# Quarter 2 of g in the last batch turned by TensorE instead of through DRAM

## The chip, the cores and the metric

One core of one Trainium2 chip runs the whole program. The metric is device time in microseconds (us): the median of several executions. One further execution ran under the hardware profiler, and every row below is from it.

## The reference, cut to what matters

Attention between tokens and a small state, a dense feed-forward layer with a piecewise activation, and a mixture of eight experts over 32 soft slots:

```python
attn = concat([softmax(x @ state.T / 8) @ state, softmax(state @ x.T / 8) @ x])   # 8 x 8 heads, 512 tokens, 32 state rows
x = attn.reshape(4352, 512)
h = x @ w_in                                                # 2048 features
g = where(h >= 1, h, where(h <= -1, 0, (h + 1) ** 2 / 4))
y = g @ w_out
logits = y @ phi                                            # 32 slots
slot_in = softmax(logits, over tokens).T @ y
slot_out = relu(slot_in @ w1[e]) @ w2[e]                    # expert e has 4 slots
out = softmax(logits, over slots) @ slot_out
```

## The kernel before

The work goes by batches b = 0 to 7 of 512 tokens each; a ninth pass, b = 8, takes the 256 state rows of all batches. In each batch `hstep` (L430) runs 16 steps m. A step makes h of 128 features x 512 tokens by six matmuls (L445; in b = 8 twelve of half the width, L453), and ScalarE, GpSimd and VectorE make g of it (the last instruction of a step is VectorE's L497). Four steps are a quarter of g: quarter k is steps 4k to 4k + 3.

g is used twice. `estep` (L554) multiplies a quarter by wp, the product of w_out and phi, into E, the logits. `smblock` (L564) makes of E the token weights dN and then, quarter by quarter, F = dN times g (L632), which VectorE adds to acc (L641). For F the tokens have to lie on the partitions, so g has to be turned, and there are two ways to do it.

The way through DRAM is `tstep` (L529). VectorE turns blocks of 32 x 32 into a buffer gD, one instruction a step (L534). After a quarter's fourth step SP issues four writes of 256 KB to DRAM (gdr, L541) and one read-back of 1 MB into nat (L543). The read-back waits in SP's queue for the writes to land, and what stands behind it waits with it.

The way by TensorE is `tquarter` (L518): 16 transposes of 128 x 128 against the identity into four PSUM tiles (gtp, L523), and four copies by ScalarE into nat or, for quarter 3, into the freed gD0.

`by_pe` (L514) says which way a quarter goes: in batches 1 to 6 all four go through DRAM; in b = 7, the last full batch, those in `CFG["pe"]` go by TensorE, here quarter 3 alone. F of b = 7 is computed during b = 8, and its quarters stand in TensorE's order between matmuls of h.

```python
def by_pe(b, c):
    return b == B or b == 0 and c not in CFG["tqv"] or b == B - 1 and c in CFG["pe"]

# in the loop, for the step mt before this one
if not by_pe(bt, mt // 4):
    tstep(bt, mt)
elif mt % 4 == 3:
    tquarter(bt, mt // 4)
```

Buffers that are no longer needed are given (L748) to loads of the experts' weights w1 (16 loads of 1 MB) and w2 (16 more). w1_0 to w1_5 go from GpSimd's queue, all later ones from SP's. gD has three buffers in turn; the third, gD2, lies in the slot wb1, which is given to w1_7. In b = 7 quarter 0 uses gD0, quarter 1 gD1 and quarter 2 gD2.

After b = 8 follow the merged slots (SI, L931), the experts' first layer (L950, reads w1), the second (SO, L983, reads w2, in two halves of eight groups), and the output: SR (L991) spreads a half of the slot outputs, and tiles `ops` (L1008) of three matmuls each are evicted, some by VectorE (L1004), some by ScalarE, and written by 16 transfers of 512 KB and 16 small ones.

The order is made by a scheduler when the program is built, except that TensorE's instructions from b = 2 up to the end of b = 7 stand as written; which of them run ahead in b = 8 and in the output is the scheduler's choice.

Of the kernel before, what the change touches and what calls it, by code (L numbers as in the profile page):

```python
# [14 lines left out]
PE = mybir.EngineType.PE  # L15


CFG = dict(hp=2000, att7=(3, 5, 6, 7, 8, 10), og=1, n3=1, n3m=12, wS=['DP', 'AD', 'AD', 'AD', 'AD', 'DP', 'AD', 'DD', 'AD', 'AD', 'AD', 'AD', 'AD', 'AD', 'AD', 'AD'], xsm=13, k0=5, rg=6, spg=0, att0=6, att=7, V0=(2, 6, 10), Vn=(0, 4, 10), Vx=12, wn='H', wsev='adad', conv=(1, 2, 3, 4, 12, 13, 19, 21, 24, 26, 28, 32, 36, 40, 44, 48, 52, 56, 60), todo=[1, 1, 1, 2, 0, 0, 0, 3, 0, 0, 2, 2, 1, 1, 0, 0], E0=2, E=1, sm=1, tqB=(5, 9, 13), GP=10, pe=(3,), psH=3, gtpX=(0, 7), tq0=(13, 15), keep=(2, 3, 4, 5), x2=(1, 1), natm=1, warm=14, bounce7=None, split=1, wt=4, so='sscscscscscscscc', smm=(1, 2, 3, 4, 5, 6, 9), tqv=(), tqvm=0, first='x', apath=2, f32c=1, place=1, attm=(3, 6, 7, 8, 9, 12), subPm=True, loDm=False, bounce=(0, 1, 2, 3), bq=('s', 's'), xq='s', nat=((1, 11), (2, 2), (2, 3), (2, 11), (3, 2), (3, 4), (3, 9), (4, 2), (4, 3), (4, 9), (5, 2), (5, 3), (5, 9), (6, 2), (6, 4), (6, 9)), subP=(), mulD=(0, 1), loD=(0, 1), qlag=0, gv0='SSSSSSSSSSSSSSSS', gv='EEESEEESEEESEEES', gvS='BBBBBBBBBBBBBBBB')


@with_exitstack
def kernel(
# [20 lines left out]
    def pool(name, bufs, **kw):  # L43
        return ctx.enter_context(tc.tile_pool(name=name, bufs=bufs, **kw))
# [6 lines left out]
    small = pool("small", 2)  # L51
    psH = pool("psH", CFG["psH"], space=PSUM)
    psE = pool("psE", 1, space=PSUM)
    psV = pool("psV", 1, space=PSUM)
    psX = pool("psX", 5 - CFG["psH"], space=PSUM)
    dram = pool("dram", 1, space=bass.MemoryType.DRAM)
# [25 lines left out]
    def slot(name, tag=None, dt=F32):  # L82
        return slots.tile([128, 2048], dt, name=name, tag=tag or name)
# [8 lines left out]

    v_s = [slot(f"v{c}", dt=F32R) if c or not CFG["f32c"] else None for c in range(2)]
    a_st = slot("ast", tag="a1")
# [27 lines left out]
    def group(calls, after=()):  # L122

        first = mm(**calls[0])  # L124
        for i in after:
            tc.add_manual_dep(first.ins, i.ins.name, SYNC, reason="side by side")
        with tc.high_priority(CFG["hp"]):
            for c in calls[1:]:
# [26 lines left out]
    def convert(src, dst, tmp):  # L155

        w = src.bitcast(U32).rearrange("p (f w) -> p f w", w=2)
        lo, hi, d = w[:, :, 0], w[:, :, 1], dst.bitcast(U32)
        nc.vector.tensor_scalar(out=d, in0=hi, scalar1=0x07FFFFFF, scalar2=3,
                                op0=ALU.bitwise_and, op1=ALU.logical_shift_left)  # L160
        nc.vector.scalar_tensor_tensor(out=d, in0=hi, scalar=0xC0000000, in1=d,
                                       op0=ALU.bitwise_and, op1=ALU.bitwise_or)
        if tmp is None:
            nc.vector.scalar_tensor_tensor(out=d, in0=lo, scalar=29, in1=d,
                                           op0=ALU.logical_shift_right, op1=ALU.bitwise_or)
        else:
            t = tmp.bitcast(U32)

            act(tmp, lo, ACTF.Relu, scale=-2.0 ** -29, bias=seven)
            act(t, tmp, ACTF.Relu, scale=-1.0, bias=seven)  # L170
            nc.vector.tensor_tensor(out=d, in0=d, in1=t, op=ALU.bitwise_or)

    def piece(i, k, dst):
        rot["t"] += 1
        tmp = None if rot["t"] in CFG["conv"] else cw_t[rot["t"] % 3]
        convert(stage[i][:, 1024 * k:1024 * k + 1024], dst, tmp)
# [33 lines left out]
    def load_x(b):  # L210
        (dma if CFG["xq"] == "s" or b < 3 else nc.gpsimd.dma_start)(out=xs_s, in_=xs[b])

# [873 lines left out]
```

## Time and profile before

| | |
|---|---|
| median of three runs | 518.12 us (517.38 to 519.41) |
| the profiled execution | 520.69 us |
| its span in the trace | 518.5 us |
| mean granted clock of TensorE | 0.944 of full speed |
| busy share of the span: TensorE, VectorE, ScalarE, GpSimd | 89%, 71%, 60%, 40% |
| HBM traffic | 100.34 MB read, 41.42 MB written |

Times in the rows are us from the span's start unless marked ns. PE is TensorE (PEld its weight loads), DVE VectorE, ACT ScalarE, POOL GpSimd, SP the engine that only issues transfers (SPq its queue). L445 is line 445. `out<-in` are the program's names, `x6` a count, and brackets at a row's end give the idle time ahead of it and what ended that.

### The profile page before, as it was taken

Reading aid. Unit: us, or ns where it says so; the run is one execution under the profiler, and the core shown is the slowest. Engines: PE = TensorE matmul, PEld = TensorE weight load, DVE = VectorE, ACT = ScalarE, POOL = GpSimd, SP = SyncE. Lnnn points to the kernel's source line nnn. Section 1 sums busy time; section 2 is a strip of 40 time slices with the busy share of each in tenths; the row PEclk is TensorE's granted clock in tenths of the full one; section 3 lists DMA queues with packets and bytes.
Section 4 is the critical chain, followed back from the end, with each engine's and each line's share of the span. In section 5 each row is a group of like instructions: output and inputs, shape, how many; then the busy total and the mean of one; then the engine's idle time right before and its main releaser. Section 6 shows DMA issues by size and latency. Waiting matters only on the chain.

```text
span 518.5 us, 9979 instructions
## 1 busy us (share of the span) xinstructions
PE 462.9 (89%) x3757; PEld 267.5 (52%) x3757; DVE 369.0 (71%) x768; ACT 313.4 (60%) x613; POOL 209.5 (40%) x211
## 2 busy tenths in 40 slices
PE   5382999999989999999998998999999769799994
PEld 2130465566545555555565455556457548335583
DVE  2999798869568879969968987985896745310370
ACT  0778997677667667767766866866656426211242
POOL 0000000045527776776776776877573100110041
PEclk9685999999999999999999999999999979989965
DMA  8998072546449797697596877789589898899998
GB/s 314 420 419 362 6 317 84 164 163 181 145 163 332 268 292 247 205 322 253 197 314 201 283 265 239 274 284 336 185 277 353 322 398 323 301 385 418 385 298 292
DMA packets 40127, 142.39 MB, mean 275 GB/s; under 512 B 3984, under 2 KB 12560, under 8 KB 27920
## 3 DMA queue, kind: packets, MB, share of 16 engines
q1 hardware_dynamic: 38400, 133.91, 72.5%
q0 software_dynamic: 1680, 7.87, 4.4%
q8 instruction: 29, 0.48, 0.4%
q14 instruction: 18, 0.15, 0.1%
HBM read 100.34 MB, written 41.42 MB: 273 GB/s over the span
## 4 chain that ended last, share of the span: by engine, by line
PE 62%; DVE 11%; DMA 7%; POOL 7%; issue 6%; ACT 5%; SPq 1%; ACTq 0%; POOLq 0%
PE h L445 24%; DMA gdr<-gD 5%; POOL v L393 4%; PE E L124 4%; PE V L124 4%; PE F L124 3%; PE h L950 3%; POOL c L475 3%; PE ops L129 3%; PE h L453 3%; PE wps L195 2%; DVE g L497 2%; ACT c L133 2%; PE gtp L523 2%; PE wtp L198 2%
## 5 line engine op out<-in xcount | busy, mean ns | idle before, releaser
L445 PE MATMUL h<-a,v 128*128 128x512 f32 x744 | 192.4, 403 | 7.1 <-DVE g L497 7.0
L445 PEld LDWEIGHTS h<-a,v 128*128 128x128 f32 x744 | 133.6, 188 | 71.2 <-DVE g L497 20.0
L475 POOL TENSOR_TENSOR c<-c 128x512 f32<-128x512 f32 x84 | 87.1, 1043 | 118.4 <-ACT c L133 117.7
L133 ACT ACTIVATE c<-h,half 128x512 f32<-128x512 f32 x128 | 87.9, 688 | 47.8 <-PE h L445 29.6
L497 DVE SCALAR_TENSOR_TENSOR g<-h,c 128x512 f32<-128x512 f32 x112 | 74.7, 671 | 36.3 <-POOL c L475 30.3
L393 POOL TENSOR_TENSOR v<-vc,v 128x512 fp32r<-128x512 f32 x48 | 61.9, 1290 | 49.6 <-ACT vc L133 49.4
L534 DVE STREAM_TRANSPOSE gD<-g 128x512 f32<-128x512 f32 x108 | 74.9, 700 | 1.8
L133 ACT ACTIVATE v<-V 128x512 fp32r<-128x512 f32 x62 | 37.1, 598 | 11.9 <-PE V L129 10.6
L124 PE MATMUL V<-win,st_t 64*32 64x512 f32 x64 | 35.9, 643 | 6.8 <-ACT att L133 5.5
L129 PE MATMUL V<-win,st_t 64*32 64x512 f32 x448 | 39.1, 636 | 0.0
L133 ACT ACTIVATE vc<-V 128x512 f32<-128x512 f32 x48 | 28.6, 596 | 15.0 <-POOL v L393 15.0
L124 PE MATMUL F<-nat,dN 128*32 128x512 f32 x54 | 26.6, 614 | 7.0 <-DMA nat<-gdr 6.6
L129 PE MATMUL E<-g,wp 128*32 128x512 f32 x168 | 29.6, 605 | 0.0
L124 PE MATMUL E<-g,wp 128*32 128x512 f32 x56 | 29.3, 605 | 0.0
L133 ACT ACTIVATE c<-c 128x512 f32<-128x512 f32 x44 | 27.8, 632 | 0.7
L129 PE MATMUL F<-nat,dN 128*32 128x512 f32 x162 | 26.8, 615 | 0.0
L453 PE MATMUL h<-XSh,v 128*128 128x256 f32 x128 | 26.1, 294 | 0.2 <-ACT nat L133 0.2
L641 DVE SCALAR_TENSOR_TENSOR acc<-acc,al,F 128x512 f32<-128x512 f32 x28 | 19.4, 724 | 7.3 <-PE F L129 7.3
L453 PEld LDWEIGHTS h<-XSh,v 128*128 128x128 f32 x128 | 20.7, 192 | 4.9 <-issue 1.7
L1036 POOL DMA_DIRECT2D out_dram<-o x16 | 7.9, 500 | 36.3 <-DVE o L1004 30.2
L129 PE MATMUL ops<-so,LC 32*128 32x256 f32 x160 | 20.6, 371 | 0.9 <-ACT o L133 0.8
L133 ACT ACTIVATE o<-ops 128x256 f32<-128x256 f32 x34 | 11.5, 381 | 15.8 <-PE ops L129 15.8
(238 smaller groups left out, 817.7 us busy)
## 6 DMA issues: line engine op xcount, KB each, us to landing
gdr<-gD SPq DMA_DIRECT2D x108, 256.0 KB, 6.8
nat<-gdr SPq DMA_DIRECT2D x27, 1024.0 KB, 6.2
w<-in_w_dram SPq DMA_DIRECT2D x24, 1024.0 KB, 10.7
xn<-in_xn_dram SPq DMA_DIRECT2D x8, 1024.0 KB, 8.6
out_dram<-o SPq DMA_DIRECT2D x16, 512.0 KB, 4.4
xs<-in_xs_dram SPq DMA_DIRECT2D x7, 1024.0 KB, 8.7
w<-in_w_dram POOLq DMA_DIRECT2D x5, 1024.0 KB, 8.9
wb<-in_win_dram SPq DMA_DIRECT2D x4, 1024.0 KB, 11.4
```

The source lines that it names most:

```text
L124: first = mm(**calls[0])
L129: e = mm(**c)
L133: return nc.scalar.activation(out=out, in_=in_, func=func, **kw)
L195: mm(out=wps[g][32 * k:32 * k + 32, :], lhsT=phi_t[:, k, :], rhs=w, start=True, stop=True)
L393: nc.gpsimd.tensor_tensor(out=lo[:, G, :], in0=vf, in1=hi[:, G, :], op=ALU.subtract)
L445: mm(out=h, lhsT=v[:, G, f], rhs=a[:, G, :], start=(k == 0), stop=(k == 5))
L453: mm(out=h, lhsT=w[:, j, :], rhs=x[:, j, :], start=(k == 0), stop=(k == 11))
L475: nc.gpsimd.tensor_tensor(out=c, in0=c, in1=c, op=ALU.mult)
L497: gI[b, m] = nc.vector.scalar_tensor_tensor(out=g, in0=h, scalar=1.0, in1=c, op0=ALU.max, op1=ALU.min)
L534: nc.vector.transpose(out=gd[:, :, :, m4, :].rearrange("p c a i -> p a c i"), in_=gT[b, m].rearrange("p (a c i) -> p a c i", a=4, i=32))
L641: nc.vector.scalar_tensor_tensor(out=a, in0=a, scalar=al, in1=F, op0=ALU.mult, op1=ALU.add)
L950: mm(out=h1[hf][32 * kt:32 * kt + 32, :], lhsT=XD[e // 4][:, kt, 32 * (e % 4):32 * (e % 4) + 32], rhs=w[kt], start=(e == 0), stop=(e == 7))
```

## The change

One entry of the table of numbers: `by_pe` now answers yes for quarter 2 of b = 7 too. Quarters 0 and 1 go through DRAM as before.

```diff
 CFG = dict(
...
-    pe=(3,),
+    pe=(2, 3),
...
 )
```

Four VectorE instructions L534, four writes L541 and one read-back L543 are gone; 16 transposes L523 and four ScalarE copies are new. The order moves at three places.

TensorE, at the turn from b = 7 to b = 8; h<-a are steps 12 to 15 of b = 7, gtp the transposes, E the logits of quarter 2, F those of batch 6, h<-XSh the first of b = 8:

```order
 L124 MATMUL F<-nat_116,dN 32x512
 L129 MATMUL F<-nat_116,dN 32x512 x3
+L445 MATMUL h<-a_819,v_123 128x512 x6
+L523 MATMUL gtp<-cst_t,g 128x128 x8
+L124 MATMUL E<-g,wp 32x512
+L129 MATMUL E<-g,wp 32x512 x3
+L523 MATMUL gtp<-cst_t,g 128x128 x8
 L445 MATMUL h<-a_819,v_123 128x512 x18
-L124 MATMUL E<-g,wp 32x512
-L129 MATMUL E<-g,wp 32x512 x3
-L445 MATMUL h<-a_819,v_123 128x512 x6
```

The transposes stand behind step 12, eight on each side of the E group, which has moved ahead of steps 13 to 15.

SP's queue, from the last quarter of batch 6 (gdr_98, nat_116) on; gdr_95 to gdr_97 and nat_113 to nat_115 are quarters 0 to 2 of batch 7, w_6 and w_7 are w1_6 and w1_7:

```order
 L541 DMA gdr_98<-gD_973 32x4x512 x4
 L543 DMA nat_116<-gdr_98 128x2048
+L724 DMA w_7_4253<-in_w_dram 128x2048
 L541 DMA gdr_95<-gD_117 32x4x512 x4
 L543 DMA nat_113<-gdr_95 128x2048
 L541 DMA gdr_96<-gD_118 32x4x512 x4
 L543 DMA nat_114<-gdr_96 128x2048
-L724 DMA w_6_4202<-in_w_dram 128x2048
-L541 DMA gdr_97<-gD_973 32x4x512 x4
-L543 DMA nat_115<-gdr_97 128x2048
-L724 DMA w_7_4238<-in_w_dram 128x2048
```

w1_7 has moved from behind quarter 2 to ahead of batch 7's quarter 0; w1_6 follows quarter 1 as before, and quarter 2's five transfers are gone.

TensorE in the second half of SO, where the output begins; before:

```order
L124 MATMUL SO<-w_9_4739,hTD 32x256
L129 MATMUL SO<-w_9_4739,hTD 32x256 x7
L991 MATMUL SR<-tail,cst_t 128x256
L124 MATMUL SO<-w_10_4745,hTD 32x256
L129 MATMUL SO<-w_10_4745,hTD 32x256 x3
L129 MATMUL SO<-w_10_4746,hTD 32x256 x2
L129 MATMUL SO<-w_10_4747,hTD 32x256 x2
L124 MATMUL SO<-w_11_4755,hTD 32x256
L129 MATMUL SO<-w_11_4755,hTD 32x256 x7
L124 MATMUL ops<-so,LC 128x256
```

And after:

```order
L124 MATMUL SO<-w_10_4760,hTD 32x256
L129 MATMUL SO<-w_10_4760,hTD 32x256 x3
L129 MATMUL SO<-w_10_4761,hTD 32x256 x2
L129 MATMUL SO<-w_10_4762,hTD 32x256 x2
L991 MATMUL SR<-tail,cst_t 128x256
L124 MATMUL SO<-w_11_4770,hTD 32x256
L129 MATMUL SO<-w_11_4770,hTD 32x256 x7
L124 MATMUL SO<-w_12_4788,hTD 32x256
L129 MATMUL SO<-w_12_4788,hTD 32x256 x7
L124 MATMUL ops<-so,LC 128x256
```

SR stands one group later and the first tiles of the output too. From there blocks of five tiles alternate with the SO groups, so four blocks instead of five stand ahead of the second SR, and 48 of the 68 tiles behind it instead of 43. The last twelve tiles in a row (before: eleven) are ScalarE's; until then the two engines take turns.

## Rows read from the trace of the kernel before

**Rows 1.** The chain that ended last, in order of time: start, length, what.

```profile
398.56 15.39 DMA gdr<-gD
```

**Rows 2.** TensorE in order of time: start, length, line, operation; around the gap.

```profile
409.05 0.59 PE L124 MATMUL F<-nat,dN 128*32 128x512 f32 x1
...
410.02 0.38 PE L453 MATMUL h<-XSh,v 128*128 128x256 f32 x1
...
412.13 0.28 PE L453 MATMUL h<-XSh,v 128*128 128x256 f32 x1
419.05 1.03 PE L124 MATMUL F<-nat,dN 128*32 128x512 f32 x1 [6.65 <-DMA nat<-gdr]
...
420.92 0.58 PE L453 MATMUL h<-XSh,v 128*128 128x256 f32 x1
...
422.50 0.66 PE L124 MATMUL F<-gD,dN 128*32 128x512 f32 x1
```

**Rows 3.** Stretches: us, busy PE PEld DVE ACT POOL, PEclk, DMA share, GB/s.

```profile
418.00:420.00 2.00, 0.95 (x8) 0.23 (x8) 0.00 (x0) 0.00 (x0) 0.00 (x0) 0.50 0.98 414
```

**Rows 4.** SP's queue in order of time; the same columns as rows 2.

```profile
373.93 3.13 SPq L541 DMA_DIRECT2D gdr<-gD  x4
382.74 0.34 SPq L543 DMA_DIRECT2D nat<-gdr  x1
383.12 2.18 SPq L541 DMA_DIRECT2D gdr<-gD  x4
395.61 0.34 SPq L543 DMA_DIRECT2D nat<-gdr  x1
...
396.92 2.11 SPq L541 DMA_DIRECT2D gdr<-gD  x4
414.08 0.34 SPq L543 DMA_DIRECT2D nat<-gdr  x1
```

**Rows 5.** DMA issues, last column us to landing: read-back at 395.61, writes from 396.92.

```profile
nat<-gdr SPq DMA_DIRECT2D x1, 1024.0 KB, 9.8
...
gdr<-gD SPq DMA_DIRECT2D x4, 256.0 KB, 14.8
```

**Rows 6.** VectorE in order of time, g of step 11 and the transposes behind it.

```profile
389.02 0.69 DVE L497 SCALAR_TENSOR_TENSOR g<-h,c 128x512 f32<-128x512 f32 x1
389.63 1.30 DVE L534 STREAM_TRANSPOSE gD<-g 128x512 f32<-128x512 f32 x2
```

**Rows 7.** TensorE around quarter 3's transposes; last, by tile: ns min/median/max, first and last start.

```profile
387.06 4.47 PE L445 MATMUL h<-a,v 128*128 128x512 f32 x18
...
395.58 0.60 PE L523 MATMUL gtp<-cst_t,g 128*128 128x128 f32 x4
395.94 0.37 PE L453 MATMUL h<-XSh,v 128*128 128x256 f32 x1
...
L523 PE MATMUL gtp<-cst_t,g x16: 271/272/273, 394.0 to 401.9; 128*128 128x128 f32 x16
```

**Rows 8.** A stretch behind step 12; the columns of rows 3.

```profile
392.00:394.00 2.00, 2.00 (x15) 1.23 (x8) 0.69 (x1) 0.28 (x1) 1.13 (x3) 1.00 1.00 413
```

**Rows 9.** The end: TensorE, then ScalarE's evictions, in order of time.

```profile
493.17 0.38 PE L124 MATMUL ops<-so,LC 32*128 32x256 f32 x1
...
494.07 0.70 PE L991 MATMUL SR<-tail,cst_t 128*128 128x256 f32 x2
...
505.39 0.66 ACT L133 ACTIVATE o<-ops 128x256 f32<-128x256 f32 x2 [0.82 <-PE ops L129]
...
512.83 0.38 ACT L133 ACTIVATE o<-ops 128x256 f32<-128x256 f32 x1 [0.78 <-PE ops L129]
```

**Rows 10.** w2_15: its issue on SP, its landing (last column), its group on TensorE.

```profile
473.56 0.33 SPq L724 DMA_DIRECT2D w<-in_w_dram  x1
...
w<-in_w_dram SPq DMA_DIRECT2D x1, 1024.0 KB, 16.9
...
492.17 0.40 PE L124 MATMUL SO<-w,hTD 128*32 128x256 f32 x1
```

More of the change, by code (lines that the diff above doesn't have):

```diff
@@ L15 @@
 PE = mybir.EngineType.PE
-CFG = dict(hp=2000, att7=(3, 5, 6, 7, 8, 10), og=1, n3=1, n3m=12, wS=['DP', 'AD', 'AD', 'AD', 'AD', 'DP', 'AD', 'DD', 'AD', 'AD', 'AD', 'AD', 'AD', 'AD', 'AD', 'AD'], xsm=13, k0=5, rg=6, spg=0, att0=6, att=7, V0=(2, 6, 10), Vn=(0, 4, 10), Vx=12, wn='H', wsev='adad', conv=(1, 2, 3, 4, 12, 13, 19, 21, 24, 26, 28, 32, 36, 40, 44, 48, 52, 56, 60), todo=[1, 1, 1, 2, 0, 0, 0, 3, 0, 0, 2, 2, 1, 1, 0, 0], E0=2, E=1, sm=1, tqB=(5, 9, 13), GP=10, pe=(3,), psH=3, gtpX=(0, 7), tq0=(13, 15), keep=(2, 3, 4, 5), x2=(1, 1), natm=1, warm=14, bounce7=None, split=1, wt=4, so='sscscscscscscscc', smm=(1, 2, 3, 4, 5, 6, 9), tqv=(), tqvm=0, first='x', apath=2, f32c=1, place=1, attm=(3, 6, 7, 8, 9, 12), subPm=True, loDm=False, bounce=(0, 1, 2, 3), bq=('s', 's'), xq='s', nat=((1, 11), (2, 2), (2, 3), (2, 11), (3, 2), (3, 4), (3, 9), (4, 2), (4, 3), (4, 9), (5, 2), (5, 3), (5, 9), (6, 2), (6, 4), (6, 9)), subP=(), mulD=(0, 1), loD=(0, 1), qlag=0, gv0='SSSSSSSSSSSSSSSS', gv='EEESEEESEEESEEES', gvS='BBBBBBBBBBBBBBBB')
+CFG = dict(hp=2000, att7=(3, 5, 6, 7, 8, 10), og=1, n3=1, n3m=12, wS=['DP', 'AD', 'AD', 'AD', 'AD', 'DP', 'AD', 'DD', 'AD', 'AD', 'AD', 'AD', 'AD', 'AD', 'AD', 'AD'], xsm=13, k0=5, rg=6, spg=0, att0=6, att=7, V0=(2, 6, 10), Vn=(0, 4, 10), Vx=12, wn='H', wsev='adad', conv=(1, 2, 3, 4, 12, 13, 19, 21, 24, 26, 28, 32, 36, 40, 44, 48, 52, 56, 60), todo=[1, 1, 1, 2, 0, 0, 0, 3, 0, 0, 2, 2, 1, 1, 0, 0], E0=2, E=1, sm=1, tqB=(5, 9, 13), GP=10, pe=(2, 3), psH=3, gtpX=(0, 7), tq0=(13, 15), keep=(2, 3, 4, 5), x2=(1, 1), natm=1, warm=14, bounce7=None, split=1, wt=4, so='sscscscscscscscc', smm=(1, 2, 3, 4, 5, 6, 9), tqv=(), tqvm=0, first='x', apath=2, f32c=1, place=1, attm=(3, 6, 7, 8, 9, 12), subPm=True, loDm=False, bounce=(0, 1, 2, 3), bq=('s', 's'), xq='s', nat=((1, 11), (2, 2), (2, 3), (2, 11), (3, 2), (3, 4), (3, 9), (4, 2), (4, 3), (4, 9), (5, 2), (5, 3), (5, 9), (6, 2), (6, 4), (6, 9)), subP=(), mulD=(0, 1), loD=(0, 1), qlag=0, gv0='SSSSSSSSSSSSSSSS', gv='EEESEEESEEESEEES', gvS='BBBBBBBBBBBBBBBB')
 @with_exitstack
```

## Prediction

> **What bounds the kernel now.** I read four views, in this order. The first is the chain of work that ended last. Most of it is TensorE in steady matmul work, but near the end of batch 7 it leaves TensorE for the DMA: one link of 15.39 us, the four writes of quarter 2 of g to DRAM, starting at 398.56 [rows 1]. No other wait in the chain is nearly as long.
>
> The second view is TensorE in order of time around that link. F of quarter 1 starts at 409.05 and gives way to the last matmuls of h at 410.02; these run out at 412.41 (412.13 + 0.28), and F of quarter 2 starts only at 419.05, after 6.65 us of waiting for the read-back of g [rows 2].
>
> The third view is busy time and clock by stretch: in 418 to 420 the granted clock is 0.50, so TensorE has fallen from 2.4 to 1.2 GHz after standing still; VectorE, ScalarE and GpSimd are busy for 0.00 of these 2 us, and only the DMA works, at 414 GB/s [rows 3]. The matmuls behind the gap pay for that too.
>
> The fourth is SP's queue. SP issues in program order and each read-back waits in the queue for its four writes to land. Quarter 0 needs 8.8 us from its first write to its read-back (373.93 to 382.74), quarter 1 12.5 us (383.12 to 395.61), quarter 2 17.2 us (396.92 to 414.08) [rows 4]. The writes of quarter 2 take 14.8 us to land, since loads of w1 go through the same DMA engines at that time [rows 5].
>
> **What goes.** The gap itself: 419.05 - 412.41 = 6.64 us. The clock behind it: F of quarter 2 takes 419.05 to 420.92 = 1.87 us, where F of quarter 1 takes 409.05 to 410.02 = 0.97, so 0.90 too long; the six matmuls of h behind it take 420.92 to 422.50 = 1.58 us, where those ahead of the gap start every 0.124 us (410.02 to 412.13 is 17 of them), so 6 x 0.124 = 0.74 and 0.84 too long [rows 2]. Together 6.64 + 0.90 + 0.84 = 8.4 us. What is late next there? F of quarter 3 comes from TensorE already, and its operand is there. Quarter 1's read-back is the only transfer still waited for, below.
>
> On VectorE four transposes go, 1.30 us for two. Two of the four stand ahead of g of step 11 (389.02 now), which therefore comes earlier or at the same time [rows 6].
>
> **What comes.** TensorE gets 16 transposes of 128 x 128, in the order behind h of step 12, eight on each side of the E group. Four such transposes for quarter 3 start at 395.58 and the next matmul starts at 395.94: 0.36 us for four, so 16 cost 1.44 us [rows 7]. They stand on TensorE's own path, which has no idle time here, so the full price counts. The fourth of the first tile needs g of step 11. Step 12 is the first third of the 18 matmuls that start at 387.06 and last 4.47, so it ends at about 388.55; g of step 11 ends at 389.02 + 0.69 = 389.71 now [rows 6, 7]. Three transposes (0.27 us) come ahead of it, so the wait is between nothing and 389.71 - 388.55 - 0.27 = 0.9 us; I take 0.2, because the two VectorE transposes that fall away were 1.30 us of what stood ahead of that g. Behind the waiting transpose stand E and h of steps 13 to 15. The E group was due anyway and only changes place: nothing. Sum: 1.6 us, between 1.4 and 2.3.
>
> The Trainium skill ("TensorE: Matmul & The Clock Gate", Part 4: PE-mode transpose) gives a 128 x 128 transpose about 275 ns in a kernel; by that the 16 would cost 4.4 us and the gain would be 3.0 us less. The trace agrees on the length of one (272 ns), but has 0.09 us from one to the next [rows 7].
>
> ScalarE gets four copies out of PSUM behind the transposes. In 392 to 394 it is busy 0.28 of 2 us and VectorE 0.69 [rows 8], so they fit beside TensorE. If that cover were gone, the third tile of transposes would wait for a copy, some tenths of a us.
>
> On SP's queue four writes and a read-back go, and one load moves. w1_7 goes to a buffer that quarter 2 no longer uses, and the order now has it ahead of all of batch 7's writes, just ahead of the writes that start at 373.93 [rows 4]. It waits for nothing, and the third write of quarter 1 waits for its landing, which is long past by then. Its issue and its 1 MB come ahead of quarter 0: at the 414 GB/s of rows 3, 1.05 MB is 2.5 us; at no price if the DMA engines have room; at worst 9.8 us, the longest landing of such a transfer [rows 5]. I take 2.5 us. Quarter 1's read-back was issued at 395.61 and landed 9.8 us later, at 405.4; its F starts at 409.05, a margin of 3.6 us [rows 2, 4, 5]. With TensorE 1.6 us later the margin is 5.2, so 2.5 us of delay is hidden, and the price is nothing. All later loads of w1 stand behind fewer bytes than before.
>
> **The end of the program.** The order also changes where nothing was meant to. SR of the first half now stands behind one more SO group, and four blocks of five output tiles stand ahead of the second SR instead of five. Now the second SR starts at 494.07 and ends about 494.77; a block ahead of it takes 493.17 to 494.07 = 0.9 us [rows 9]. Behind it 43 tiles remain until 512.83 + 0.38 = 513.21. The last eleven are evicted by ScalarE alone, from 505.39 on: 7.8 us, 0.71 each; the 32 ahead of them take 505.39 - 494.77 = 10.6 us, 0.33 each [rows 9]. Now 48 tiles will remain, 36 and then twelve for ScalarE alone: 4 x 0.33 + 0.71 = 2.0 us more, less the block of 0.9 that no longer stands ahead: 1.1 us, which I round to 1.0, between nothing and 2.0.
>
> **Sum.** 8.4 - 1.6 - 1.0 = 5.8 us. The profiled execution took 520.69 us (span 518.5 and 2.2 around it), so such a one would take 514.9. The median of the runs is 518.12; 518.12 - 5.8 = 512.3.
>
> **Rivals.** *Quarter 1 is late.* The wait moves from quarter 2 to quarter 1. If quarter 1's writes take as long as quarter 2's did (17.2 us), its read-back goes at 383.12 + 2.5 + 17.2 = 402.8 and lands at 412.6; its F is due at 410.65, TensorE waits 2.0 us: 514.3. For it: the same DMA engines carry w1 loads. Against it: the margin of 5.2 us, and that quarter 1 took 12.5.
>
> *No overlap among the transposes.* [...] Each of the 16 waits for the one before it to end: 16 x 0.272 = 4.35 us [rows 7], 2.9 more than 1.44, so 515.2. Against it: four of them in 0.36 us.
>
> *The weights bind the end.* w2_15 is issued at 473.56, lands 16.9 us later at 490.5, and its group starts at 492.17 [rows 10]. If the DMA engines are the bound from w1 to there, it lands at 490.5 whatever TensorE does; the group then starts 1.7 us earlier than now and the end pays 1.0 to 2.0: 517.4 to 518.4, no change. Against it: the load's issue waits for buffers that TensorE frees, so it moves with TensorE, and two megabytes are gone from the queue.
>
> *Slower.* One mechanism, the load put ahead of both round trips on SP. If with w1_7 in front both take as long as quarter 2's did, 17.2 us each, quarter 0's read-back goes at about 374.8 + 17.2 = 392.0 and quarter 1's at 392.4 + 17.2 = 409.6, landing at 419.4. TensorE then waits 8.75 us for quarter 1 and pays the 1.74 us of clock again: 512.3 + 10.5 = 522.8. It decides from a landing later than 410.65 + 5.8 = 416.5, 11 us later than now. Against it: one transfer of 1 MB doing the work of four.
>
> **How the numbers follow.** The forecast has 0.76, with a range of its own of 510.6 to 514.0 (tail between nothing and 2.0, transposes up to 2.3, and a clock that may fall or rise a us or so elsewhere at the end). Quarter 1 late 0.08, no overlap among the transposes 0.04, weights bind 0.08, slower 0.04. This kernel's runs can tell about 0.5%, that is 2.6 us: below 515.5 is faster. Faster: 0.76 + 0.08 + 0.04 = 0.88; same 0.08; slower 0.04. The range goes from the forecast's low end to 515.5 and leaves out the last two rivals.
>
> **What would show it.** In the profile after: no gap on TensorE ahead of F of quarter 2, and a clock of 1.00 from 390 to 430; 16 transposes between step 12 and step 13 in about 1.5 us, with at most a short wait for g; quarter 1's read-back landing before its F; the span from the end of F of quarter 3 to the first SO about as long as now; twelve tiles in single file at the end, and the stretch from the second SR to the last eviction about 20.4 us instead of 18.4. I am wrong if F of quarter 1 or an SO group waits for a DMA, or if TensorE's clock falls elsewhere.

## The result, and the profile after

| | before | after |
|---|---|---|
| median beside each other, 7 executions each | 519.41 us (517.38 to 525.18) | 513.83 us (513.47 to 515.33) |
| ratio | | 0.9885, 95% interval 0.9854 to 0.9916 |
| profiled execution, and its span | 520.69, 518.5 us | 514.06, 511.8 us |
| mean granted clock there | 0.944 | 0.957 |
| all executions of this study | 80 beside the variants: median 519.4, from 511.7 to 524.2 | 17: median 514.1, from 513.5 to 516.0 |

Faster by 5.3 to 5.6 us, or 1.1%. The kernel before scatters over 12 us from one execution to the next, without parting into two groups, and the kernel after over 2.5, so the experiments below are given by the medians of all their executions. They were timed in four rounds, in which the median of before is 518.96 to 519.61. A ratio that leaves out executions more than 1.5% above a kernel's fastest drops 15 of the 29 of before in one round and so makes the difference there 0.9964 (0.9926 to 1.0001), where the medians of all are 514.47 and 519.61.

First the place the prediction was about. TensorE in order of time (start, length, line, operation, count, idle time ahead), the first F of quarters 0, 2 and 3:

```profile
408.82 0.62 PE L124 MATMUL F<-nat,dN 128*32 128x512 f32 x1 [0.37 <-ACT dN L133]
...
412.98 0.62 PE L124 MATMUL F<-nat,dN 128*32 128x512 f32 x1
...
414.89 0.62 PE L124 MATMUL F<-gD,dN 128*32 128x512 f32 x1
```

Where [rows 2] have 6.65 us of waiting ahead of F of quarter 2, nothing stands in brackets at 412.98. The stretches (columns of [rows 3]) have the clock that goes with it:

```profile
414.00:418.00 4.00, 4.00 (x36) 3.03 (x33) 3.50 (x9) 1.53 (x3) 0.00 (x0) 1.00 0.71 250
418.00:420.00 2.00, 2.00 (x22) 1.45 (x21) 1.93 (x9) 1.40 (x4) 0.00 (x0) 1.00 1.02 401
```

TensorE is busy throughout and at 1.00 of full speed (2.4 GHz), where [rows 3] had 0.50 (1.2 GHz).

Next, what was added, TensorE at the turn to b = 8:

```profile
385.83 1.66 PE L445 MATMUL h<-a,v 128*128 128x512 f32 x6
387.32 1.27 PE L523 MATMUL gtp<-cst_t,g 128*128 128x128 f32 x8
388.52 0.62 PE L124 MATMUL E<-g,wp 128*32 128x512 f32 x1
...
389.51 1.09 PE L523 MATMUL gtp<-cst_t,g 128*128 128x128 f32 x8
390.36 4.39 PE L445 MATMUL h<-a,v 128*128 128x512 f32 x18
...
394.73 0.36 PE L453 MATMUL h<-XSh,v 128*128 128x256 f32 x1
```

The second eight transposes take 389.51 to 390.36 = 0.85 us, 0.106 each. The first eight take 387.32 to 388.52 = 1.20, so 0.35 of it is the wait for g of step 11.

SP's queue, from the last read-back of batch 6 on, as in [rows 4]:

```profile
369.89 0.34 SPq L543 DMA_DIRECT2D nat<-gdr  x1
370.27 0.43 SPq L724 DMA_DIRECT2D w<-in_w_dram  x1
370.75 2.15 SPq L541 DMA_DIRECT2D gdr<-gD  x4
380.90 0.34 SPq L543 DMA_DIRECT2D nat<-gdr  x1
381.28 2.32 SPq L541 DMA_DIRECT2D gdr<-gD  x4
394.71 0.34 SPq L543 DMA_DIRECT2D nat<-gdr  x1
```

The load at 370.27 is w1_7. Behind it quarter 0's round trip takes 10.2 us (8.8 in [rows 4]) and quarter 1's 13.4 (12.5), and F of quarter 1 waits for nothing.

The chain of work that ended last has two links of DMA now, both loads of w2, near the end:

```profile
450.82 15.30 DMA w<-in_w_dram
466.18 17.00 DMA w<-in_w_dram
```

They are behind two short waits of TensorE in the second half of SO; with them the second SR (compare [rows 9, 10]):

```profile
480.75 0.40 PE L124 MATMUL SO<-w,hTD 128*32 128x256 f32 x1 [0.51 <-DMA w<-in_w_dram]
...
483.22 0.41 PE L124 MATMUL SO<-w,hTD 128*32 128x256 f32 x1 [0.51 <-DMA w<-in_w_dram]
...
485.15 0.70 PE L991 MATMUL SR<-tail,cst_t 128*128 128x256 f32 x2
```

And the last evictions, the first and the last of the twelve in single file on ScalarE:

```profile
496.73 0.38 ACT L133 ACTIVATE o<-ops 128x256 f32<-128x256 f32 x1 [0.47 <-PE ops L129]
...
504.80 0.38 ACT L133 ACTIVATE o<-ops 128x256 f32<-128x256 f32 x1 [0.24 <-PE ops L129]
```

Put together by stage, from the starts of these and the like rows; the two columns "again" are the second traces taken in the experiments:

| stage, us | before | before again | after | after again |
|---|---|---|---|---|
| up to the last F of batch 6 | 386.52 | 386.17 | 385.29 | 386.93 |
| from there to the first h of b = 8 (has the transposes) | 7.57 | 7.57 | 9.44 | 9.40 |
| from there to the last F of quarter 3 (has the gap) | 28.91 | 27.76 | 20.61 | 20.63 |
| from there to SI, and SI to the experts' first layer | 33.19 | 33.39 | 33.49 | 33.49 |
| the first layer (L950) | 15.59 | 15.59 | 13.90 | 13.89 |
| from there to SO | 2.50 | 2.50 | 2.50 | 2.51 |
| SO to the second SR | 19.79 | 21.48 | 19.92 | 20.45 |
| second SR to the last eviction | 19.14 | 18.35 | 20.03 | 19.82 |
| last eviction to the end of the span | 5.29 | 6.29 | 6.62 | 6.58 |

Between the first traces: -1.23 +1.87 -8.30 +0.30 -1.69 +0.13 +0.89 +1.33 = -6.7, the difference of the spans. The first and the fifth number were in nobody's sum, and the experiments have to say whether they belong to the change.

### The profile page after: what moved, and what is told of

Same layout as the page of the kernel before. It is cut to its first block, busy times and chain, and to the rows that moved or that the text cites. A ratio compares the mean times of both kernels' runs of the same rounds, so it can differ in the third digit from the quotient of the medians.

```text
span 511.8 us, 10000 instructions
## 1 busy us (share of the span) xinstructions
PE 461.1 (90%) x3773; PEld 271.1 (53%) x3773; DVE 366.2 (72%) x764; ACT 316.1 (62%) x617; POOL 209.5 (41%) x211
## 4 chain that ended last, share of the span: by engine, by line
PE 61%; DVE 12%; POOL 8%; DMA 7%; issue 6%; ACT 4%; SPq 0%; POOLq 0%; ACTq 0%
PE h L445 24%; DMA w<-in_w_dram 6%; PE h L453 5%; PE E L124 4%; POOL v L393 4%; PE V L124 4%; PE F L124 3%; PE ops L129 3%; POOL c L475 3%; PE gtp L523 3%; PE wps L195 2%; DVE g L497 2%; PE wtp L198 2%; DVE win L161 2%; ACT c L133 1%
## 5 line engine op out<-in xcount | busy, mean ns | idle before, releaser
L534 DVE STREAM_TRANSPOSE gD<-g 128x512 f32<-128x512 f32 x104 | 72.2, 700 | 1.8
L124 PE MATMUL V<-win,st_t 64*32 64x512 f32 x64 | 34.2, 615 | 6.9 <-ACT att L133 5.5
L129 PE MATMUL V<-win,st_t 64*32 64x512 f32 x448 | 37.9, 616 | 0.0
L124 PE MATMUL F<-nat,dN 128*32 128x512 f32 x54 | 25.8, 598 | 0.4 <-ACT dN L133 0.4
L129 PE MATMUL F<-nat,dN 128*32 128x512 f32 x162 | 26.0, 598 | 0.0
L129 PE MATMUL ops<-so,LC 32*128 32x256 f32 x160 | 21.9, 382 | 0.0
L133 ACT ACTIVATE o<-ops 128x256 f32<-128x256 f32 x34 | 12.5, 382 | 14.4 <-PE ops L129 14.3
L124 PEld LDWEIGHTS V<-win,st_t 64*32 64x32 f32 x64 | 4.4, 106 | 30.1 <-issue 18.2
```

The source lines that it names most:

```text
L129: e = mm(**c)
L133: return nc.scalar.activation(out=out, in_=in_, func=func, **kw)
L534: nc.vector.transpose(out=gd[:, :, :, m4, :].rearrange("p c a i -> p a c i"), in_=gT[b, m].rearrange("p (a c i) -> p a c i", a=4, i=32))
```

## The experiments

**Both ways at once, F from TensorE.** Does the gain come from the wait, from the 2 MB less, or from w1_7 having moved? The kernel after keeps the way through DRAM, unread; the read-back goes into gD2 itself (that line is left out here):

```diff
...
                 elif mt % 4 == 3:
                     tquarter(bt, mt // 4)
+                if bt == B - 1 and mt // 4 == 2:
+                    tstep(bt, mt)
```

> The kernel after with quarter 2's way through DRAM kept as well: four VectorE transposes, four writes of 256 KB and the read-back of 1 MB, whose result nothing reads. TensorE's order is that of after, SP's that of before. Wait theory (the gain is TensorE's wait for the read-back that is gone): F of quarter 2 starts without a gap, the granted clock stays at 1.00 there, and the time is that of after, 513.8 us, plus 0 to 3 us for loads of weights that come later. Traffic theory (the gain is the 2 MB that no longer go through the DMA engines): about 519 us, as before. Load theory (the gain is w1_7 having moved ahead of the round trips): about 519 us too.

Measured 515.79 us (514.32 to 520.59, 12 executions) beside 519.52 for before. SP's queue and TensorE:

```profile
393.89 3.13 SPq L541 DMA_DIRECT2D gdr<-gD  x4
412.35 0.34 SPq L543 DMA_DIRECT2D gD<-gdr  x1
```

```profile
414.38 0.62 PE L124 MATMUL F<-nat,dN 128*32 128x512 f32 x1
```

The round trip takes 18.5 us until the read-back goes, and that lands 4.8 us later, at 417.1; F starts at 414.38 and does not care. So most of the gain stays with all the traffic in place and w1_7 in its old place. The traffic and load theories do not hold for the bulk.

**Both ways at once, F from DRAM.** The counterpart, the kernel before with the transposes added. In the first version the four copies went to a buffer q that the order had meant for a 256 KB piece of w1_3, which so moved behind them; in the second they stay in PSUM:

```diff
+                if (bt, mt) == (B - 1, 11):
+                    tquarter(bt, 2)
...
-            act(nat_of(b, k)[:, t], tp)
+            act(tp if (b, k) == (B - 1, 2) else nat_of(b, k)[:, t], tp)
```

> The kernel before, with the 16 transposes and four copies of the kernel after added (into a buffer that nothing reads); F of quarter 2 still reads what comes back from DRAM. SP's order is that of before, TensorE's end that of after. Wait theory: the added 2 us of TensorE's time lie inside the gap ahead of F of quarter 2, which shrinks from 6.6 to about 4.6 us; the time is that of before, 519.4 us, plus 0 to 1 for the end's order. Theory that a TensorE instruction always adds its time: 519.4 + 2.1 = 521.5 or more.

> As the run both_read_dram (16 transposes on TensorE, F of quarter 2 from DRAM, SP's order that of before), but the four copies behind the transposes now stay in PSUM, so GpSimd's 256 KB piece of w1_3 is issued as early as in the kernel before; in both_read_dram it had moved behind the copies, out of the way of quarter 1's writes. If that piece made the gap go there: the gap ahead of F of quarter 2 is back, 2 to 5 us long, and the time is 518 to 520. If the transposes' time alone covers the wait: no gap or one below 1 us, and 516.4 as there.

Measured 516.36 (514.66 to 524.21) for the first, where I had expected 519.4 to 520.4, and 519.44 (515.43 to 521.34) for the second, beside 519.61. SP and TensorE in the trace of the second:

```profile
391.43 2.98 SPq L541 DMA_DIRECT2D gdr<-gD  x4
409.26 0.34 SPq L543 DMA_DIRECT2D nat<-gdr  x1
```

```profile
415.41 0.62 PE L124 MATMUL F<-nat,dN 128*32 128x512 f32 x1
```

The traced execution was the luckiest of its twelve (515.43): its read-back went at 409.26, landed 5.0 us later and 1.1 us before F. Three of the twelve executions stand between 515.4 and 516.3, one at 518.0 and eight between 519.3 and 521.3. That these have the gap is argued, not seen. As a median, 16 transposes on TensorE's own path cost nothing that shows (519.44 beside 519.61) as long as the read-back is what ends last. Against both_read_pe, which runs the same instructions in nearly the same order and differs in what F waits for, the wait is worth 519.44 - 515.79 = 3.7 us.

**The piece alone.** The first version raised a suspicion: is the early 256 KB piece the cause of the gap? The kernel before, with only that piece held back:

```diff
+                if (bt, mt) == (B - 1, 11):
+                    for t in range(4):
+                        act(rot_q.tile([128, 512], F32, tag="q", name="q"), gT[bt, 8 + t])
```

> The kernel before, all four quarters of its way unchanged, with one thing moved: the 256 KB piece of w1_3 is issued about 10 us later, since its buffer is held by four ScalarE copies of g that nothing reads. No transposes. If the piece delays quarter 1's writes and with them, down SP's queue, quarter 2's read-back: quarter 1's round trip takes 9 us instead of 12.5, the gap ahead of F of quarter 2 shrinks from 6.6 to about 3 us, and the time is 516 to 517.5. If the round trips only vary from execution to execution: the gap and the time stay, 519.4.

Measured 519.42 (516.86 to 522.48). Quarter 1's round trip was 10.0 us, near what I had written, but quarter 2's took 20.4 and F waited 6.54 us. The suspicion fell: the piece is worth nothing by itself, and what quarter 1 gains quarter 2 can lose. Why the first version came out 3 us below the second stays open.

**Before and after once more.** Both unchanged, for a second trace.

> The kernel before, profiled once more. If the late read-back of batch 6 (373.55 in the first trace, 3 us after its place in the traces of the variants) was of that execution alone: it is at 370 to 371, the gap ahead of F of quarter 2 is 3 to 5 us instead of 6.65, and the time 517 to 519. If it belongs to the kernel: 373.5 again, and 6.6.

> The kernel after, profiled once more and timed beside the variants. By the wait theory no gap ahead of F of quarter 2, as in its first trace, and 513.8. If the full clock during the experts' first layer (13.9 us there instead of 15.6) belongs to the change: 13.9 again; if it is of the execution: 15.6 may come.

Before: 521.27 us. TensorE at F of quarter 2, and SP's round trip for it:

```profile
417.20 1.03 PE L124 MATMUL F<-nat,dN 128*32 128x512 f32 x1 [5.14 <-DMA nat<-gdr]
```

```profile
393.55 3.04 SPq L541 DMA_DIRECT2D gdr<-gD  x4
412.28 0.34 SPq L543 DMA_DIRECT2D nat<-gdr  x1
```

The last read-back of batch 6 went at 371.38 instead of 373.55 and the gap was 5.14 instead of 6.65 us, yet the execution took longer. So the size of the gap is of the execution, its presence of the kernel. After: 514.47 (513.45 to 515.96, ten executions) beside 519.61, again no gap, and the first layer again in 13.9 us.

**Without the transposes.** What do they cost, and does it reach the end?

```diff
+            if (b, k) == (B - 1, 2):
+                act(nat_of(b, k)[:, t], gT[b, 4 * k + t])
+                continue
```

> The kernel after without the 16 transposes of quarter 2: ScalarE copies g itself into nat2, so F of quarter 2 is made of unturned data (left out: the turn). SP's queue and TensorE's order are otherwise those of after. If the transposes cost what the trace of after shows between step 12 and step 13, 2.1 us, and all of it reaches the end: 513.8 - 2.1 = 511.7. By the prediction's 1.6: 512.2. If the end is bound by the weights' loads, little of it reaches the end: 513.3 or more.

Measured 512.31 (512.28 to 514.18, six executions). TensorE:

```profile
386.08 4.39 PE L445 MATMUL h<-a,v 128*128 128x512 f32 x18
390.40 0.62 PE L124 MATMUL E<-g,wp 128*32 128x512 f32 x1
...
391.40 1.66 PE L445 MATMUL h<-a,v 128*128 128x512 f32 x6
...
393.02 0.36 PE L453 MATMUL h<-XSh,v 128*128 128x256 f32 x1
```

The stage is 7.48 us long instead of 9.44 and 9.40, so the transposes cost 1.9, and the medians differ by 514.1 - 512.3 = 1.8. By the medians the price is paid in full and all of it reaches the end. The spans of single traces would not show it: this one has the slower first layer (15.6 us, below) and 45.2 us from SO to the end instead of 46.6.

**VectorE's transposes kept.** The kernel after with quarter 2's four L534, but no DMA; this also puts w1_7 back behind the round trips:

```diff
+                if bt == B - 1 and mt // 4 == 2:
+                    tstep(bt, mt)
...
-        if m4 == 3:
+        if m4 == 3 and not by_pe(b, c):
```

> The kernel after with quarter 2's four VectorE transposes kept (nothing reads them), without its writes and read-back. That holds the buffer gD2, and so puts w1_7 back behind batch 7's round trips on SP; TensorE's order is that of after. Wait theory: as after, 513.8, within 1 us. Load theory: about 519. If the four VectorE transposes that fell away were what brought g of step 11 early: a wait of up to 0.9 us among the 16 transposes, so 514 to 514.7.

Measured 515.24 (514.33 to 517.32). TensorE's first eight transposes:

```profile
387.33 0.49 PE L523 MATMUL gtp<-cst_t,g 128*128 128x128 f32 x3
388.55 0.76 PE L523 MATMUL gtp<-cst_t,g 128*128 128x128 f32 x5 [0.73 <-DVE g L497]
```

The fourth transpose waits 0.73 us for g of step 11, since two VectorE transposes stand ahead of that g; the stage grows to 10.12 us, 0.7 more than in after. Of the 1.1 us between 515.24 and 514.1 this is 0.7, and w1_7's place is worth at most the other 0.4. both_read_pe has the same longer stage, so of its 1.7 us above after 0.7 are this wait too, and the 2 MB of traffic and w1_7's place together have at most the other 1.0.

**Less of w1.** Why does quarter 2 take 17 to 20 us through DRAM? The kernel before, all its own ways kept, but with 2.25 MB less loaded at that time:

```diff
+            if kind == "w1" and i in (1, 2, 4):
+                (nc.gpsimd if 2 < state["next"] < CFG["GP"] else nc.sync).dma_start(out=ts[0][:, 0:512], in_=src[:, 0:512])
+                where[kind, i] = place, [parts[0]] * 4
...
```

> The kernel before with one thing left out: of three loads of w1 on GpSimd's queue (w1_1, w1_2, w1_4) only a quarter each is loaded and used four times, 2.25 MB less in the DMA engines while quarters 1 and 2 of batch 7 are on their way through DRAM. No transposes; SP's order is that of before, TensorE's too but for the output at the end, which is that of after. If it is the loads of w1 that make quarter 2's round trip 17 to 19 us long: it takes about 12, the gap ahead of F of quarter 2 is below 2 us or gone, and the time is 512 to 515. If SP's queue is late for another reason: the gap stays at 5 to 6.6 us and the time at 519 to 520.5.

Measured 513.62 (511.60 to 514.54, six executions) beside 519.51. SP, then TensorE:

```profile
390.12 2.02 SPq L541 DMA_DIRECT2D gdr<-gD  x4
403.14 0.34 SPq L543 DMA_DIRECT2D nat<-gdr  x1
```

```profile
411.50 0.62 PE L124 MATMUL F<-nat,dN 128*32 128x512 f32 x1
```

The round trip is 13.0 us, where before took 17.2 and 18.7; the read-back lands 7.0 us later at 410.2, F does not wait, and the time is that of after without the 16 added transposes on TensorE. So it is the loads of w1, from another engine's queue, that make the writes late. The Trainium skill ("DMA: Bandwidth & Descriptors", Issuing engines are not separate DMA queues) says that transfers from all engines' queues end up on the same 16 DMA engines and interleave there; this run agrees.

**Quarter 1 as well.** One more quarter by TensorE:

```diff
 CFG = dict(
...
-    pe=(2, 3),
+    pe=(1, 2, 3),
...
 )
```

> The kernel after with quarter 1 turned by TensorE as well; quarter 0 alone goes through DRAM in batch 7. In the trace of after no F waits for quarter 1, so by the wait theory there is nothing left to gain and the 16 further transposes cost their 1.9 us in full: 514.2 + 1.9 = 516.1, less up to 0.7 where fewer VectorE transposes bring g earlier. Traffic theory (each 2 MB less are worth 1 to 2 us at the end): 514 or less.

Measured 514.60 (514.47 to 514.92, six executions), beside 518.96 for before. That is neither the 515.4 to 516.1 of the wait theory nor 514 or less, and not faster than after. TensorE ahead of step 12 of b = 7, first in the second trace of after, then here:

```profile
377.50 4.38 PE L445 MATMUL h<-a,v 128*128 128x512 f32 x18
...
383.16 1.66 PE L445 MATMUL h<-a,v 128*128 128x512 f32 x6 [1.28 <-DVE g L497]
...
387.46 1.66 PE L445 MATMUL h<-a,v 128*128 128x512 f32 x6
```

```profile
376.88 1.65 PE L445 MATMUL h<-a,v 128*128 128x512 f32 x6
378.37 1.04 PE L523 MATMUL gtp<-cst_t,g 128*128 128x128 f32 x8
...
379.79 1.14 PE L523 MATMUL gtp<-cst_t,g 128*128 128x128 f32 x8 [0.39 <-ACT nat L133]
...
387.68 1.66 PE L445 MATMUL h<-a,v 128*128 128x512 f32 x6
```

In after this stretch has a wait of 1.28 us for VectorE's g. With four VectorE transposes fewer it is gone, and the stretch grows only from 9.96 to 10.80 us. I had allowed 0.7 of 1.9 for that, and 1.1 fell away; the new transposes lie partly in a wait again.

**The clock in the first layer.** Five small matmuls in the waits ahead of it:

```diff
+    for _ in range(2):
+        mm(out=wm, lhsT=ident, rhs=P[:, 0:128], start=True, stop=True)
     SI = psX.tile([128, 512], F32, tag="X", name="SI")
...
```

> The kernel after with five small matmuls added that nothing reads, in TensorE's three waits ahead of the experts' first layer (0.75, 0.81 and 0.37 us). That layer took 13.9 us in both traces of after and 15.6 in four others, where the granted clock fell to 0.50 for some 3.5 us. If standing still in those waits is what lets the clock fall: 13.9 us in every execution, and a median up to 0.7 us below that of after with less scatter. If not: the scatter stays and the time is that of after, 514.2.

Measured 515.01 (513.41 to 515.30, six executions): no gain and no less scatter. The layer without a drop of the clock (here) and with one (ve_kept):

```profile
450.19 13.96 PE L956 MATMUL h<-w,tail 128*32 128x512 f32 x128
```

```profile
449.54 15.66 PE L952 MATMUL h<-w,tail 128*32 128x512 f32 x128 [0.37 <-ACT tail L133]
```

```profile
449.00:454.00 5.00, 4.63 (x30) 1.33 (x33) 0.00 (x0) 0.34 (x2) 0.00 (x0) 0.66 1.01 389
```

In 449 to 454 of ve_kept the granted clock has a mean of 0.66. Of the 14 traces, four have this drop: both of before, no_transposes and ve_kept. piece_late has the gap and no drop, ve_kept and no_transposes have no gap and a drop. So a gap alone does not bring the drop, and none is needed for it; the expected remedy shows no effect on the time. Whether the drop goes by the execution or by the kernel stays open: both traces of before have it, neither trace of after, and no kernel was seen with and without.

**Less of w2.** Do the weights bind the end of after? Its last four loads of w2 by a quarter each:

```diff
+            if kind == "w2" and i >= 12:
+                nc.sync.dma_start(out=ts[0][:, 0:512], in_=src[:, 0:512])
+                where[kind, i] = place, [parts[0]] * 4
...
```

> The kernel after, with only a quarter of each of the last four loads of w2 (the quarter is used four times; left out: 3 MB of weights). SO and output tiles come in another order at the end, their number is the same. If the DMA engines bind the end (they were busy all of the last 30 us in after, and two SO groups waited 0.5 us each for w2): from SO's start to the end of the span 42 us or less instead of 46.7, and 510 or less. If the evictions of output tiles bind it: 45.5 to 46.5 us, and 513 to 514.

Measured 513.78 (513.66 to 516.30, five executions). No SO group waits for w2 and the second SR comes 17.33 us behind SO's start instead of 19.92, but from SO to the end of the span it is 46.4 us, against 46.6 and 46.9. A stretch near the end, first of this kernel, then of after:

```profile
490.00:500.00 10.00, 9.84 (x82) 8.91 (x76) 5.76 (x15) 5.32 (x14) 2.60 (x6) 0.50 1.03 328
```

```profile
490.00:500.00 10.00, 10.00 (x82) 9.70 (x80) 5.66 (x15) 5.09 (x14) 2.51 (x6) 0.50 1.00 319
```

They are alike: TensorE busy at 1.2 GHz with 82 matmuls, and the DMA engines full with output. The end is bound by the output tiles, not by weights. Whether it is their matmuls at 1.2 GHz, their evictions or their transfers, the runs do not separate.

## Why the prediction was right

The forecast was 512.3 us, the result 513.83, inside the forecast's own range and near its upper end of 514.0. By its steps:

- **The gap and the clock behind it.** 8.4 us predicted. All traces without a gap take 20.61 to 20.64 us from the first h of b = 8 to F of quarter 3, so in the first trace the gap and its clock were 28.91 - 20.61 = 8.30. Right for that execution; in before again it was 7.14 and in piece_late 8.57. What the prediction did not have is that the writes' 14.8 us and with them the gap vary by execution.
- **The transposes.** 1.6 predicted, between 1.4 and 2.3. Measured 1.87 (9.44 - 7.57) and 1.83; the term was a little small, since one transpose follows the other at 0.106 us instead of 0.09 and the wait for g was 0.35 instead of 0.2. That makes 2.05 us; the 24 matmuls of h around them took 0.17 less than before. That two VectorE transposes falling away keep this wait short is shown by ve_kept. The 1.30 us of [rows 6] that the prediction used for them belong to the two behind that g. The rival without overlap (4.35 us) did not come.
- **w1_7's move.** Hidden, as predicted: at most 0.4 us. Quarter 1's read-back landed 8.4 us behind 394.71, at 403.1, 6.6 us before its F; in after again, with a round trip of 15.6 us, it landed at 408.5, 2.8 us before. The margin is real but not wide.
- **The end.** +1.0 predicted, between nothing and 2.0. In the first pair of traces it was +0.13 +0.89 +1.33 = 2.35, in the second +0.7 (46.85 against 46.12). Over the three traces with before's order of the end (44.22, 46.12 and 44.50) and the eight with after's and nothing left out (45.55 to 47.29, mean 46.4) it is 1.4. The parts differ from the working: the block that no longer stands ahead of the second SR (-0.9) was eaten by the two waits for w2 (2 x 0.51), the stretch behind the second SR grew by 0.9 instead of 2.0, and 1.3 came behind the last eviction, which the prediction left out. An SO group that waits for a DMA was one of the prediction's own signs of being wrong, and in the first trace of after it came, twice; w2_quarter shows that these waits cost nothing in the end. The rival in which weights bind fails too: w2_15 landed at 466.18 + 17.00 = 483.18, not at 490.5. The rise of 1.4 comes from traces that differ by 2 us among themselves; it is smaller than the gap's worth and did not hold it back.
- **Not in any step.** The first layer's 1.7 us and the 1.2 us up to batch 6. The second goes with the granted clock in the first 60 us, which also differs between the two traces of after (0.83 and 0.77 there, 385.29 and 386.93 us in the table). Neither is shown to belong to the change.
- **The median.** The prediction took its 5.8 from a median of three executions, 518.12; 80 more have a median of 519.4. The difference came out as 519.4 - 514.1 = 5.3, and by stages with the mean of three traces of before: -8.0 + 1.85 + 1.4 = -4.7, so some 0.6 us of it stay unassigned, within what clock and round trips vary. Luck has a part in how near the number came: the three terms as measured give 4.7 where the prediction had 5.8. Of the 1.5 us between 512.3 and 513.83, 1.3 are the median that it started from (519.41 beside the result).

The mechanism holds: TensorE waited for a round trip through DRAM, and turning the quarter itself costs less than the wait. Two runs sharpen it. The same wait goes, and the same time comes out, if the loads that crowd the writes are thinned (w1_quarter); and it can go by luck, as in the trace of both_read_dram2 at 515.4 (the execution of before at 511.7 has no trace). The change buys independence from this round trip for 1.9 us of TensorE. That this is also why its executions lie within 2.5 us where those of before lie within 12 is likely, but no run shows it by itself.

## What to carry to other kernels

The length of a wait for a round trip through DRAM is a number of one execution (5.14 to 6.65 us in three traces here, and none in the trace of both_read_dram2): take a second trace before sizing it. Work added to the engine that waits is free up to the length of the wait and costs its full price once the wait is gone (nothing that shows and 1.9 us here for the same 16 transposes). Before moving work to the busiest engine, look at what shares the DMA engines with the late transfer; here 2.25 MB of loads beside it were worth as much as the whole change.

## What the hardware showed that I had not expected

The granted clock can fall where nothing near it in the program differs. In before, ve_kept, piece_late and after the waits ahead of the first layer are the same (0.75, 0.81 and 0.37 us), and yet the layer runs in 15.6 us in the first two and in 13.9 in the others. The Trainium skill ("TensorE: Matmul & The Clock Gate", Part 1) says that what watches the activity runs free and is not in step with a kernel, which would give such a lottery; no run here shows it.

In batch 7 the same 1 MB of writes took from 8.3 us (quarter 0 in before again) to 20.4 us (quarter 2 in piece_late) until its read-back went, with 256 KB pieces landing in 5.8 us (both_read_dram2) to 18.6 us (piece_late).
